# Column units among row units: PV with V as weights, row sums of P by adds on Pool and VectorE

## The chip, the core and the metric

The kernel runs on one core of a Trainium2 chip. Its engines work side by side, each with its own queue, in the order in which the instructions were written into it: TensorE (PE in the profile, its weight loads PEld), VectorE (DVE), ScalarE (ACT), GpSimd (Pool) and SyncE (SP), which here issues most of the DMA transfers. The metric is the device time of one execution in microseconds. Three runs of the kernel before took 1303.82, 1303.84 and 1304.23 us; the median is 1303.84.

## What is computed

Two parts follow each other on x, of 2048 rows by 512 columns: attention with a cached K and V, and a gated MLP that mixes rows. Both are framed by a LayerNorm and a modulation that comes from a small vector c. Cut to what matters here:

```python
h = layernorm(x) * (1 + ca) + sa
q = h @ wq                                  # 32 heads of 128, 2048 rows
scores = q @ k^T * Dh ** (-0.5)             # 4 heads of q share one of 8 K/V groups, 2048 keys
p = softmax(scores, axis=-1)
x = x + ga * ((p @ v) as [2048, 4096] @ wo)
# then: x = x + gb * mixer(layernorm(x) * (1 + cb) + sb)
```

In the kernel the softmax takes no maximum off; it takes exp of the scaled scores, and the sum of each row's exps divides what comes out of PV or of the output projection. A flag at the end guards the sums: if one is out of bounds, the whole is computed again by a general path, which does not run on these inputs.

## The kernel before, in words

Attention is cut into 128 units: 8 K/V groups times 16 tiles of 128 query rows. One unit is 4 heads by 128 queries against 2048 keys, which are 16 key tiles. The loop over `it` has one iteration for each unit's scores, and each iteration has 8 slots. In a slot TensorE does a pair of score matmuls of 512 columns into a PSUM tile of two banks (`s_ps`, two of them), and ScalarE takes the exp of that pair. Into the same slots the loop interleaves PV of an earlier unit (`pv_part`), one matmul of the q projection for a later block (`fill`, slots 0 to 3 of nearly every iteration), and one matmul of the output projection of a still earlier unit (`wo_proj`, slots 4 to 7). The order on each engine's queue is written out by hand: what is emitted first stands first, and `at(it, slot, fn)` puts a function at the head of a later slot. The tile library adds the waits on semaphores and hands out buffers.

There are two kinds of units.

- A row unit keeps q as the weights, so P comes out with queries on partitions (`qk`, line 1021). The exp (line 1028) delivers the sums of its rows by the way, and `turn_rows` adds two halves of them on VectorE (`tot`, line 1082) and takes the reciprocal (line 1085). P has to be turned by a DMA transpose on SP's queue. PV then has V as weights and streams P: 16 matmuls of 512 columns (`pv_rows`, line 1093), which give the output already transposed; VectorE copies it out of PSUM into `oT` (line 1102). As the sums are not yet divided out, each head's output projection goes to a PSUM bank of its own, and VectorE scales and adds it into `xacc` (line 1164).
- A column unit keeps K as the weights, so P comes out with keys on partitions (line 1058, exp at line 1065) and need not be turned. PV takes P as weights, tile by tile, and streams V with a column of ones behind it: 64 matmuls of 129 columns (`pv`, line 1114). The 129th column is the sum. VectorE takes the reciprocals (line 1125) and normalises (line 1126), a DMA transpose turns the result into `oT`, and the four heads of the output projection add up in one PSUM bank, which VectorE adds to `xacc` (line 1158).

Units 5 to 121 repeat row, row, column. A row unit's PV comes 2 or 3 iterations after its scores and a column unit's 1 after, so each iteration holds one PV; the output projection follows 3 iterations behind PV. The iteration after a column unit's therefore has scores of a row unit, PV of the column unit, and the output projection of the column unit before it.

PSUM has eight banks: four for the two `s_ps`, two named `o_ps` for PV, and two named `misc`, which the q projection and the output projection share. The q projection's bank is emptied by VectorE's cast into `qT` (line 970). Pool has next to nothing to do until the last group, when it multiplies and adds the finished rows (lines 1187 and 1188).

Of the kernel before, what the change touches and what calls it, by code (L numbers as in the profile page):

```python
# [10 lines left out]
BF16 = mybir.dt.bfloat16  # L11
FP32 = mybir.dt.float32
ACT = mybir.ActivationFunctionType
ALU = mybir.AluOpType
AX = mybir.AxisListType
P = 128
# [559 lines left out]
def kernel(  # L576
# [19 lines left out]
    nc = tc.nc  # L596
    _, S, D = A_x.shape
    _, HKV, SK, DH = A_k_cache.shape
    HQ = A_wq.shape[1] // DH
    REP = HQ // HKV  # L600
# [4 lines left out]
    NT = S // P  # L605
    NDT = D // P
    NKT = SK // P
# [5 lines left out]
    NSLOT = NKT // 2  # L613
# [26 lines left out]
    res = fast.enter_context(tc.tile_pool(name="res", bufs=1))  # L640
# [4 lines left out]
    late = free_b.enter_context(tc.tile_pool(name="late", bufs=2, side="right"))  # L645
# [24 lines left out]
    def bank(name):  # L670
        return psum.tile([P, 512], FP32, name=name)

    def bank2():
        return psum.tile([P, 1024], FP32, name="s_ps")
# [11 lines left out]
    def normalise(dst, src, mv, rstd):  # L686
        nc.vector.tensor_scalar(
            out=dst,
            in0=src,
            scalar1=mv,  # L690
            scalar2=rstd,
            op0=ALU.subtract,
            op1=ALU.mult,
        )
# [215 lines left out]
    for dt in range(NDT):  # L910
        dst, src = hTs[0][:, dt, 0:P], xT0[:, dt * P : (dt + 1) * P]
        if dt == 1:
            nc.scalar.activation(
                out=dst,
# [67 lines left out]
    def by_rows(u):  # L982
        return TURN_A <= u < TURN_B and (u - TURN_A) % len(LAGS) < len(LAGS) - 1

    row_units = [u for u in range(NU) if by_rows(u)]

    def pv_at(u):
# [15 lines left out]
    def at(it, slot, fn):  # L1003
        later.setdefault((it, slot), []).append(fn)

    def qk(u, i):
        g, j = divmod(u, NT)
        b, jj = g * NCH + j // CT, j % CT
        if i == 0:
            if homes[u] == "wsp":  # L1010
                pTs[u] = wspp.tile([P, NT, 512], BF16, name="wsp")
            else:
                pTs[u] = late.tile([P, NKT, 512], BF16, name=homes[u], bufs=1)
            if by_rows(u):
                rsums[u] = stat.tile([P, NSLOT], FP32, name="rs")
        s_ps = bank2()
        if by_rows(u):
            hh, half = divmod(i, 2)
            for c in range(2):
                k0 = (2 * half + c) * 512  # L1020
                nc.tensor.matmul(  # L1021
                    s_ps[:, c * 512 : (c + 1) * 512],
                    lhsT=qTs[b][:, hh, jj * P : (jj + 1) * P],
                    rhs=groups[g]["kT"][:, k0 : k0 + 512],
                    start=True,
                    stop=True,
                )
            nc.scalar.activation(  # L1028
                out=rows_of(u, hh)[:, half * HK : (half + 1) * HK],
                in_=s_ps[:],  # L1030
                func=ACT.Exp,
                scale=inv_sqrt_dh,
                accum_out=rsums[u][:, i : i + 1],
            )
            if half == 1:
                at(*divmod(u * NSLOT + i + 1, NSLOT), lambda: turn_rows(u, hh))
            return
        if u < 2:
            pair, k0 = i // 4, i % 4 * 4
            qs = slice(pair * 256, (pair + 1) * 256)  # L1040
            for kt in range(4):
                nc.tensor.matmul(  # L1042
                    s_ps[:, kt * 256 : (kt + 1) * 256].rearrange("p (r q) -> p r q", r=2),
                    lhsT=groups[g]["kT"][:, (k0 + kt) * P : (k0 + kt + 1) * P],
                    rhs=qTs[b][:, 2 * pair : 2 * pair + 2, jj * P : (jj + 1) * P],
                    start=(kt % 2 == 0),
                    stop=(kt % 2 == 1),
                )
            nc.scalar.activation(
                out=pTs[u][:, k0 : k0 + 4, qs],  # L1050
                in_=s_ps[:].rearrange("p (k q) -> p k q", k=4),
                func=ACT.Exp,
                scale=inv_sqrt_dh,
            )
            return
        for h in range(2):
            kt = 2 * i + h
            nc.tensor.matmul(  # L1058
                s_ps[:, h * 512 : (h + 1) * 512].rearrange("p (r q) -> p r q", r=REP),
                lhsT=groups[g]["kT"][:, kt * P : (kt + 1) * P],  # L1060
                rhs=qTs[b][:, :, jj * P : (jj + 1) * P],
                start=True,
                stop=True,
            )
        nc.scalar.activation(  # L1065
            out=pTs[u][:, 2 * i : 2 * i + 2, :],
            in_=s_ps[:].rearrange("p (k q) -> p k q", k=2),
            func=ACT.Exp,
            scale=inv_sqrt_dh,
        )  # L1070

    def rows_of(u, hh):
        return pn[(row_units.index(u) * REP + hh) % len(pn)][:, 0:SK]
# [71 lines left out]

    def wo_proj(u):
        g, j = divmod(u, NT)
        each = by_rows(u)
        ps = {}

        def into(first, X_ps, scale):
            if first:
                xaccs[j] = late.tile([P, D], FP32, name=f"xacc{j}", bufs=1)
            xa = xaccs[j]
            if scale is None and first:
                nc.vector.tensor_copy(out=xa[:], in_=X_ps[:])
            elif scale is None:
                nc.vector.tensor_tensor(out=xa[:], in0=X_ps[:], in1=xa[:], op=ALU.add)
            elif first:
                nc.vector.tensor_scalar(  # L1160
                    out=xa[:], in0=X_ps[:], scalar1=scale, scalar2=None, op0=ALU.mult
                )
            else:
                nc.vector.scalar_tensor_tensor(  # L1164
                    out=xa[:], in0=X_ps[:], scalar=scale, in1=xa[:], op0=ALU.mult, op1=ALU.add
                )

        def mm(hh):
            if hh == 0 or each:
                ps[0] = bank("misc")  # L1170
            nc.tensor.matmul(  # L1171
                ps[0][:],
                lhsT=oTs[u][:, hh, :],
                rhs=groups[g]["wo"][:, hh, :],
                start=(hh == 0 or each),
                stop=(hh == REP - 1 or each),
            )
            if each:
                c0 = u * REP + hh
                into(g == 0 and hh == 0, ps[0], rall[:, c0 : c0 + 1])  # L1180
            elif hh == REP - 1:
                into(g == 0, ps[0], None)
            if hh < REP - 1 or g < HKV - 1:
                return
            xa = xaccs[j]
            engine = nc.gpsimd if j < NT - CT else nc.vector
            engine.tensor_tensor(out=xa[:], in0=xa[:], in1=ga_rows[:], op=ALU.mult)
            engine.tensor_tensor(
                out=x_sb[:, j, :], in0=xa[:], in1=x_sb[:, j, :], op=ALU.add
            )  # L1190
            if j >= NT - CT:
                ln_stats(mv2, j, x_sb[:, j, :])

        return [lambda hh=hh: mm(hh) for hh in range(REP)]

    def ln2(it, j):

        st = {}

        def first():  # L1200
            if j < NT - CT:
                ln_stats(mv2, j, x_sb[:, j, :])
            st["rstd"] = rstd_of(mv2[:, j : j + 1, :], 1, "ln2")

        def second():
            xn = res.tile([P, D], BF16, name="xn2", bufs=2)
            normalise(xn[:], x_sb[:, j, :], mv2[:, j, 0:1], st["rstd"][:, 0:1])
            st["xnT"] = res.tile([P, NDT, P], BF16, name="xnT2", bufs=2)
            nc.sync.dma_start_transpose(out=st["xnT"][:], in_=xn[:])

        def third():
            ch, c0 = j // CT, (j % CT) * P
            if ch not in h2Ts:
                h2Ts[ch] = res.tile([P, NDT, 512], BF16, name="hT", bufs=NCH)
            for dt in range(NDT):
                nc.vector.tensor_scalar(
                    out=h2Ts[ch][:, dt, c0 : c0 + P],
                    in0=st["xnT"][:, dt, :],
                    scalar1=modc[:, 4 * NDT + dt : 4 * NDT + dt + 1],
                    scalar2=modc[:, 3 * NDT + dt : 3 * NDT + dt + 1],  # L1220
                    op0=ALU.mult,
                    op1=ALU.add,
                )

        at(it + 1, 0 if j >= NT - CT else 2, first)
        at(it + 1, 4, second)
        at(it + 2, 3, third)
# [44 lines left out]
        first[j] = ln1_stats(j, 1)  # L1272

    def tile_norm(j):
        xn = res.tile([P, D], BF16, name="xn2", bufs=2)
        normalise(xn[:], x_sb[:, j, :], mv1[:, j, 0:1], first[j][:, 0:1])
        first[j] = xn

# [193 lines left out]
        at(NU + 5, 5 + ch, lambda ch=ch: z2_norm(ch))  # L1472

    def pv_part(u, i, n):
        if by_rows(u):
            return pv_rows(u, i, n)
        for k in range(NSLOT // n):
            pv(u, i * (NSLOT // n) + k)
# [250 lines left out]
```

## Time and profile before

| | |
|---|---|
| median of three runs | 1303.84 us |
| profiled execution | 1303.83 us |
| its span, first to last instruction | 1302.0 us |
| TensorE busy | 1287.0 us, 99% |
| ScalarE busy | 1112.8 us, 85% |
| VectorE busy | 685.7 us, 53% |
| Pool busy | 59.0 us, 5% |
| main DMA queue, share of 16 engines | 87.5% |

The page of a profile gives busy times of each engine, the chain of work that ended last, and the costliest groups of instructions. A timeline row gives the start in microseconds from the span's start, the duration, engine, line, operation, what is written and read with the shape, and how many instructions were merged; in brackets stands the idle time of that engine before it and what ended it. A row of groups gives the count, the busy time, the mean duration of one in nanoseconds, and after the last bar the idle time ahead of them. A matmul's duration reaches to the modelled end of its way through the array; the next starts earlier than that, so time on TensorE is best read from one start to another.

### The profile page before, as it was taken

The numbers are of one execution on the slowest core, as the hardware profiler recorded it, in microseconds if no ns is written. First come the engines' busy times: TensorE is split into PE (matmuls) and PEld (weight loads), VectorE is DVE, ScalarE is ACT, GpSimd is POOL, SyncE is SP. The second block draws the span as 40 slices with busy tenths as digits, with TensorE's granted clock in tenths as the row PEclk, the third lists the DMA queues.
The fourth block names the chain that finished last, engine by engine and source line by source line (L and its number), as shares of the span: only waits on it lengthen the run. The fifth ranks groups of instructions, "written<-read, shape, count | busy, mean of one in ns | idle before, by whom it ended". The sixth has DMA issues, their size and how long they took to land.

```text
span 1302.0 us, 22572 instructions
## 1 busy us (share of the span) xinstructions
PE 1287.0 (99%) x8512; PEld 700.2 (54%) x8665; DVE 685.7 (53%) x1777; ACT 1112.8 (85%) x1683; POOL 59.0 (5%) x99
## 2 busy tenths in 40 slices
PE   9999999999999999999999999999999999999998
PEld 7655555555555555555555555555555556644445
DVE  7545455545554555455545554555455566784444
ACT  7999999999999999999999999999999998650000
POOL 2000000000000000000000000000000133410000
PEclk9999999999999999999999999999999999999999
DMA  7999999999999999999999999999999973254300
GB/s 207 183 188 181 168 184 191 190 166 188 189 181 177 186 174 189 183 171 188 190 175 181 187 192 181 169 195 173 176 193 165 172 146 91 49 138 98 81 21 32
DMA packets 774997, 211.18 MB, mean 162 GB/s; under 512 B 759264, under 2 KB 773216, under 8 KB 774880
## 3 DMA queue, kind: packets, MB, share of 16 engines
q1 hardware_dynamic: 772864, 207.94, 87.5%
q10 hardware_dynamic: 2016, 1.71, 0.4%
q8 instruction: 70, 1.15, 0.4%
q14 instruction: 47, 0.39, 0.1%
HBM read 21.37 MB, written 2.10 MB: 18 GB/s over the span
## 4 chain that ended last, share of the span: by engine, by line
PE 98%; issue 1%; ACT 1%; DMA 0%; SPq 0%; DVE 0%; ACTq 0%
PE s_ps L1021 21%; PE o_ps L1093 20%; PE o_ps L1114 14%; PE s_ps L1058 13%; PE misc L1171 8%; PE misc L959 8%; PE misc L1573 7%; PE s_ps L1397 2%; PE s_ps L1436 2%; PE o_ps L1606 1%; PE s_ps L1042 0%; PE s_ps L1606 0%; DMA kT<-in_A_k_cache_dram 0%; ACT pn L1028 0%; ACT win_sb L1028 0%
## 5 line engine op out<-in xcount | busy, mean ns | idle before, releaser
L1021 PE MATMUL s_ps<-kT,qT 128*128 128x512 bf16 x1219 | 365.0, 379 | 2.3
L1028 ACT ACTIVATE win_sb<-s_ps 128x1024 bf16<-128x1024 f32 x312 | 319.0, 1023 | 3.4 <-PE s_ps L1021 0.7
L1093 PE MATMUL o_ps<-pT,v 128*128 128x512 bf16 x909 | 272.6, 379 | 1.5
L1164 DVE SCALAR_TENSOR_TENSOR xacc<-misc,rall,xacc 128x512 f32<-128x512 f32 x304 | 227.5, 748 | 69.2 <-PE misc L1171 61.7
L1058 PE MATMUL s_ps<-qT,kT 128*128 128x512 bf16 x768 | 228.4, 379 | 0.8
L1065 ACT ACTIVATE pT<-s_ps 128x1024 bf16<-128x1024 f32 x208 | 209.8, 1024 | 11.8 <-PE s_ps L1058 3.6
L1028 ACT ACTIVATE pn<-s_ps 128x1024 bf16<-128x1024 f32 x208 | 212.7, 1023 | 2.3 <-PE s_ps L1021 0.7
L1093 PEld LDWEIGHTS <-v 128*128 128x128 bf16 x1248 | 121.9, 98 | 147.9 <-issue 1.1
L1065 ACT ACTIVATE wsp<-s_ps 128x1024 bf16<-128x1024 f32 x176 | 179.8, 1023 | 12.4 <-PE s_ps L1058 4.6
L1171 PE MATMUL misc<-wo_g,oT 128*128 128x512 bf16 x479 | 181.6, 379 | 1.0
L1021 PEld LDWEIGHTS <-qT 128*128 128x128 bf16 x1248 | 121.4, 98 | 109.4 <-issue 0.4
L959 PE MATMUL misc<-hT,wq_g 128*128 128x512 bf16 (+1 forms) x499 | 178.3, 369 | 0.5
L970 DVE CAST qT<-misc 128x512 bf16<-128x512 f32 x126 | 86.5, 687 | 153.5 <-PE misc L959 153.5
L1114 PEld LDWEIGHTS <-pT 128*128 128x128 bf16 x1792 | 119.6, 98 | 48.8
L1082 DVE TENSOR_TENSOR tot<-rs 128x1 f32<-128x1 f32 x312 | 48.4, 155 | 171.3 <-ACT win_sb L1028 114.9
L1114 PE MATMUL o_ps<-v,pT 128*128 128x129 bf16 x1792 | 137.5, 220 | 0.6
L1058 PEld LDWEIGHTS <-kT 128*128 128x128 bf16 x768 | 74.1, 98 | 81.1 <-issue 1.1
L1114 PEld LDWEIGHTS <-wsp 128*128 128x128 bf16 x1408 | 94.3, 98 | 41.5
L1114 PE MATMUL o_ps<-v,wsp 128*128 128x129 bf16 x1408 | 108.5, 220 | 0.5
L1028 ACT ACTIVATE wmod_a<-s_ps 128x1024 bf16<-128x1024 f32 x104 | 106.3, 1023 | 0.6 <-PE s_ps L1021 0.4
L1573 PE MATMUL misc<-wsp,z 128*128 128x512 bf16 (+2 forms) x554 | 100.1, 336 | 0.3
L1093 PE MATMUL o_ps<-wsp,v 128*128 128x512 bf16 x292 | 87.8, 379 | 0.4
(118 smaller groups left out, 894.6 us busy)
## 6 DMA issues: line engine op xcount, KB each, us to landing
wo_g<-in_A_wo_dram SPq DMA_DIRECT2D x8, 512.0 KB, 4.5
wq_g<-in_A_wq_dram SPq DMA_DIRECT2D x7, 512.0 KB, 4.1
v<-in_A_v_cache_dram SPq DMA_DIRECT2D x7, 512.0 KB, 4.7
wsp<-in_w_mod_dram SPq DMA_DIRECT2D x1, 2048.0 KB, 9.1
pT<-win_sb SPq DMA_TRANSPOSE x117, 5.0
win_sb<-in_B_w_in_dram SPq DMA_DIRECT2D x1, 1792.0 KB, 7.3
x_sb<-in_A_x_dram SPq DMA_DIRECT2D x3, 512.0 KB, 7.0
out_dram<-yout ACTq DMA_DIRECT2D x12, 128.0 KB, 1.7
```

The source lines that it names most:

```text
L959: nc.tensor.matmul(ps[0][:, o0 : o0 + n], lhsT=wqs[g][:, dt, hh * DH : (hh + 1) * DH], rhs=hTs[ch][:, dt, c0 : c0 + n], start=(dt == 0), s ...
L970: nc.vector.tensor_copy(out=dst, in_=src)
L1021: nc.tensor.matmul(s_ps[:, c * 512 : (c + 1) * 512], lhsT=qTs[b][:, hh, jj * P : (jj + 1) * P], rhs=groups[g]["kT"][:, k0 : k0 + 512], sta ...
L1028: nc.scalar.activation(out=rows_of(u, hh)[:, half * HK : (half + 1) * HK], in_=s_ps[:], func=ACT.Exp, scale=inv_sqrt_dh, accum_out=rsums[u ...
L1058: nc.tensor.matmul(s_ps[:, h * 512 : (h + 1) * 512].rearrange("p (r q) -> p r q", r=REP), lhsT=groups[g]["kT"][:, kt * P : (kt + 1) * P], ...
L1065: nc.scalar.activation(out=pTs[u][:, 2 * i : 2 * i + 2, :], in_=s_ps[:].rearrange("p (k q) -> p k q", k=2), func=ACT.Exp, scale=inv_sqrt_dh,)
L1082: nc.vector.tensor_tensor(out=tot[:], in0=rs[:, 2 * hh : 2 * hh + 1], in1=rs[:, 2 * hh + 1 : 2 * hh + 2], op=ALU.add)
L1093: nc.tensor.matmul(o_pss[u][:], lhsT=groups[g]["v1"][:, kt, 0:DH], rhs=pTs[u][:, kt, :], start=(kt == 0), stop=(kt == NKT - 1),)
L1114: nc.tensor.matmul(o_ps[:, hh % 2, 0 : DH + 1], lhsT=pTs[u][:, kt, hh * P : (hh + 1) * P], rhs=groups[g]["v1"][:, kt, 0 : DH + 1], start=( ...
L1164: nc.vector.scalar_tensor_tensor(out=xa[:], in0=X_ps[:], scalar=scale, in1=xa[:], op0=ALU.mult, op1=ALU.add)
L1171: nc.tensor.matmul(ps[0][:], lhsT=oTs[u][:, hh, :], rhs=groups[g]["wo"][:, hh, :], start=(hh == 0 or each), stop=(hh == REP - 1 or each),)
L1573: nc.tensor.matmul(g_pss[f][:, :n], lhsT=z2[:, st, f * P : (f + 1) * P], rhs=wsp[t][:, st, c0 : c0 + n], start=(st == 0), stop=(st == NT - ...
```

## The change

For the 35 column units u = 7, 10, ... 109 (`by_sums`), PV is done as for row units: V as weights, P streamed in 16 matmuls of 512 columns, the result copied straight into `oT`. The normalising operations on VectorE, the DMA transpose of `onorm` and the column of ones go out of use for them, and their output projection becomes one PSUM bank and one scaled add on VectorE per head.

The sums of P are made by adds. Pool adds key tiles 0 to 11 into one float tile of 128 x 512 (11 operations, emitted in slots 1 to 6 of the unit's own iteration), VectorE adds tiles 12 to 15 into another (3 operations, at the head of slots 0, 1 and 2 of the next iteration). Pool joins the two into a bf16 tile (`join`), and in slot 2 of the iteration after that four matmuls of one column, with this tile as weights and ones streamed, add it over the partitions (`close`); VectorE takes the reciprocals. The two float tiles (`acc`) take the place of the second LayerNorm's buffers, which now live in tiles of the same name.

In the excerpts of the change, lines of `add`'s and `close`'s arguments are shortened to one line.

```diff
+    def by_sums(u):
+        return TURN_A <= u < (HKV - 1) * NT and not by_rows(u)
...
+            if by_sums(u):
+                key_sums(u)
...
+    N_POOL = 12
+
+    def key_sums(u):
+        acc = [res.tile([P, D], FP32, name="acc", bufs=2) for _ in range(2)]
+        pT = pTs[u]
+
+        def add(engine, a, kt, first):
+            engine.tensor_tensor(out=a[:],
+                in0=pT[:, first, :] if kt == first + 1 else a[:], in1=pT[:, kt, :], op=ALU.add)
+
+        for kt in range(1, N_POOL):
+            at(*divmod(u * NSLOT + kt // 2 + 1, NSLOT), lambda kt=kt: add(nc.gpsimd, acc[0], kt, 0))
+        for kt, (unit, slot) in zip(range(N_POOL + 1, NKT), ((1, 0), (1, 1), (1, 2))):
+            at(u + unit, slot, lambda kt=kt: add(nc.vector, acc[1], kt, N_POOL))
+
+        def join():
+            onorms[u] = late.tile([P, REP, P], BF16, name="onorm", bufs=3)
+            nc.gpsimd.tensor_tensor(out=onorms[u][:], in0=acc[0][:]..., in1=acc[1][:]..., op=ALU.add)
+
+        def close():
+            t_ps = bank("o_ps")
+            for hh in range(REP):
+                nc.tensor.matmul(t_ps[:, hh : hh + 1], lhsT=onorms[u][:, hh, :],
+                    rhs=ones_bf[:, 0:1], start=True, stop=True)
+            nc.vector.reciprocal(out=rall[:, u * REP : (u + 1) * REP], in_=t_ps[:, 0:REP])
+
+        at(u + 1, 4, join)
+        at(u + 2, 2, close)
...
     def wo_proj(u):
         g, j = divmod(u, NT)
-        each = by_rows(u)
+        each = by_rows(u) or by_sums(u)
...
     def pv_part(u, i, n):
-        if by_rows(u):
+        if by_rows(u) or by_sums(u):
             return pv_rows(u, i, n)
```

More of the change, by code (lines that the diff above doesn't have):

```diff
@@ L1070, in qk @@
         )
+    N_POOL = 12
[3 more added lines that the diff above has]
+        def add(engine, a, kt, first):
+            engine.tensor_tensor(
+                out=a[:],
+                in0=pT[:, first, :] if kt == first + 1 else a[:],
+                in1=pT[:, kt, :],
+                op=ALU.add,
+            )
+        for kt in range(1, N_POOL):
[4 more added lines that the diff above has]
+            onorms[u] = late.tile([P, REP, P], BF16, name="onorm", bufs=3)
+            nc.gpsimd.tensor_tensor(
+                out=onorms[u][:],
+                in0=acc[0][:].rearrange("p (r q) -> p r q", r=REP),
+                in1=acc[1][:].rearrange("p (r q) -> p r q", r=REP),
+                op=ALU.add,
+            )
+        def close():
+            t_ps = bank("o_ps")
+            for hh in range(REP):
+                nc.tensor.matmul(
+                    t_ps[:, hh : hh + 1],
+                    lhsT=onorms[u][:, hh, :],
+                    rhs=ones_bf[:, 0:1],
+                    start=True,
+                    stop=True,
+                )
+            nc.vector.reciprocal(out=rall[:, u * REP : (u + 1) * REP], in_=t_ps[:, 0:REP])
+        at(u + 1, 4, join)
+        at(u + 2, 2, close)
     def rows_of(u, hh):
@@ L1205, in second @@
         def second():
[L1206 to L1209, printed above, removed]
+            both = res.tile([P, D], FP32, name="acc", bufs=2)[:].bitcast(BF16)
+            xn = both[:, 0:D]
+            normalise(xn, x_sb[:, j, :], mv2[:, j, 0:1], st["rstd"][:, 0:1])
+            st["xnT"] = both[:, D : 2 * D].rearrange("p (d q) -> p d q", d=NDT)
+            nc.sync.dma_start_transpose(out=st["xnT"], in_=xn)
         def third():
@@ L1274, in tile_norm @@
     def tile_norm(j):
-        xn = res.tile([P, D], BF16, name="xn2", bufs=2)
+        xn = res.tile([P, D], FP32, name="acc", bufs=2)[:].bitcast(BF16)[:, 0:D]
         normalise(xn[:], x_sb[:, j, :], mv1[:, j, 0:1], first[j][:, 0:1])
```

## The prediction

> **What bounds the kernel now.** I read the page's busy times and its chain first, then the engines' timelines through one period of the attention stage, then the groups by shape. The profiled execution took 1303.83 us, of which 1302.0 are the span; it agrees with the median of the runs, 1303.84, so sums against it stand as they are. About 0.2% (2.6 us) is what a measurement of this kernel can tell from no change.
>
> ```profile
> span 1302.0 us, 22572 instructions
> PE 1287.0 (99%) x8512; PEld 700.2 (54%) x8665; DVE 685.7 (53%) x1777; ACT 1112.8 (85%) x1683; POOL 59.0 (5%) x99
> PE 98%; issue 1%; ACT 1%; DMA 0%; SPq 0%; DVE 0%; ACTq 0%
> ```
>
> TensorE is the bound, without gaps. Whatever takes a microsecond out of its stream saves one, and whatever makes it wait costs one. VectorE is half idle and Pool almost wholly: the work that the change gives them is free on average, and costs only where TensorE waits for it. So the question is which of their instructions TensorE waits for, and when.
>
> The order repeats every three units: two row units, one column unit. One unit's scores take 8 slots. Call the iteration of a column unit's own scores C, and the next two R1 and R2. R1 holds the column unit's PV. From TensorE's timeline (start us, duration, what, count):
>
> ```profile
> 605.22 0.59 PE L1021 MATMUL s_ps<-kT,qT 128*128 128x512 bf16 x2
> 613.85 0.59 PE L1058 MATMUL s_ps<-qT,kT 128*128 128x512 bf16 x2
> 620.11 0.38 PE L1171 MATMUL misc<-wo_g,oT 128*128 128x512 bf16 x1
> 622.49 0.59 PE L1021 MATMUL s_ps<-kT,qT 128*128 128x512 bf16 x2
> 622.92 0.62 PE L1114 MATMUL o_ps<-v,pT 128*128 128x129 bf16 x8
> 631.29 0.59 PE L1021 MATMUL s_ps<-kT,qT 128*128 128x512 bf16 x2
> ```
>
> C starts at 613.85, R1 at 622.49 and the next R2 at 631.29. With a row unit's PV inside, an iteration lasts 622.49 - 613.85 = 8.64 us (605.22 to 613.85: 8.63); R1, with the 64 narrow PV matmuls, 8.80. In a row-PV iteration the second output matmul (slot 5) stands at 620.11, 6.26 us after the start. I need this below.
>
> **The change, part by part.**
>
> *PV of 35 column units* (u = 7, 10, ... 109): 64 matmuls of 129 columns become 16 of 512, so R1 should shrink to the others' length: 8.80 - 8.64 = 0.16 us, 35 times, -5.6 us.
>
> *Four one-column matmuls per unit* come in on TensorE. The nearest row is the modulation's, 16 of the same form:
>
> ```profile
> 59.02 0.54 PE L839 MATMUL o_ps<-sc_bf,wsp 128*128 128x1 bf16 x16
> 59.42 0.59 PE L1021 MATMUL s_ps<-kT,qT 128*128 128x512 bf16 x2
> ```
>
> 16 take 59.42 - 59.02 = 0.40 us, 25 ns each, so four take 0.10 us; 35 times +3.5 us. TensorE's own gain is therefore only 0.06 us a unit, 2.1 in all. They use an o_ps bank, and the built program gives them the one that the column unit's PV left a slot or two earlier, and the PV two iterations later takes that one again: no bank is asked for while its copy is running, so I take nothing for it (had it been the other bank, the 0.69 us oT copy would stick out by some 0.3 us, 10 us in all).
>
> *Moved off:* 35 transposes of onorm leave SP's queue and 35 x (2 reciprocals, 2 normalising operations) leave VectorE. The chain has DMA at 0% and SP's queue at 0%, so this gains nothing; nothing else is moved past a queue. The exps and the row units' transposes stay. LayerNorm's buffers at the end merely change their name and share a tile, at the same depth: nothing.
>
> *Output projection of these units:* each head now has its own PSUM bank and its own VectorE operation (748 ns) in place of one sum (681). It falls into R1, slots 4 to 7, as the row units' does elsewhere at one slot each without holding TensorE up. But two misc banks now alternate in R1 between the q projection (slots 0 to 3) and the four heads. The second head's matmul takes the bank that the q cast (L970) has to empty, the third the bank of the first head's L1164. Before, one bank served all four heads. So in R1 TensorE newly waits for VectorE's queue at slot 5, 6.26 us in.
>
> *What now stands in that queue before the q cast:* three adds of P (L1084 in the changed kernel) and the row sum "tot". And Pool does 11 adds and a join. The prices, from the groups by shape (busy us, mean ns of one):
>
> ```profile
> L1164 DVE SCALAR_TENSOR_TENSOR xacc<-misc,rall,xacc 128x512 f32<-128x512 f32 x304 | 227.5, 748 | 69.2 <-PE misc L1171 61.7 <-PE s_ps L1058 0.9
> L970 DVE CAST qT<-misc 128x512 bf16<-128x512 f32 x126 | 86.5, 687 | 153.5 <-PE misc L959 153.5
> L1102 DVE CAST oT<-o_ps 128x512 bf16<-128x512 f32 x78 | 53.9, 691 | 11.9 <-PE o_ps L1093 3.6
> L1085 DVE RECIPROCAL rall<-tot 128x1 f32<-128x1 f32 x312 | 51.1, 164 | 10.8
> L1082 DVE TENSOR_TENSOR tot<-rs 128x1 f32<-128x1 f32 x312 | 48.4, 155 | 171.3 <-ACT win_sb L1028 114.9 <-ACT pn L1028 55.4
> L1158 DVE TENSOR_TENSOR xacc<-misc,xacc 128x512 f32<-128x512 f32 x42 | 28.6, 681 | 3.6 <-PE misc L1171 2.4 <-PE s_ps L1058 1.2
> L1065 ACT ACTIVATE pT<-s_ps 128x1024 bf16<-128x1024 f32 x208 | 209.8, 1024 | 11.8 <-PE s_ps L1058 3.6
> L1187 POOL TENSOR_TENSOR xacc<-xacc,ga_rows 128x512 f32<-128x512 f32 x12 | 15.3, 1276 | 215.6 <-DVE xacc L1158 180.4 <-DVE xacc L1164 35.2
> L1188 POOL TENSOR_TENSOR x_sb<-xacc,x_sb 128x512 bf16<-128x512 f32 x12 | 13.8, 1154 | 0.9
> L1187 DVE TENSOR_TENSOR xacc<-xacc,ga_rows 128x512 f32<-128x512 f32 x4 | 2.8, 692 | 0.1
> ```
>
> A VectorE add is 0.69 us (its L1187). A Pool add lies between 1.15 and 1.28 us (float and bf16 inputs, with a bf16 or a float output); I take 1.22. Added up without interference, R1's queue is fine: 3 x 0.69 = 2.1 us of adds start about 1.3 us in and end by 3.4, before the q cast is even due (4.5 us in: 618.37 - 613.85, below).
>
> Interference is what decides, and the trace shows it where Pool's L1187/L1188 run beside VectorE:
>
> ```profile
> 1022.84 1.27 POOL L1187 TENSOR_TENSOR xacc<-xacc,ga_rows 128x512 f32<-128x512 f32 x1 [165.43 <-DVE xacc L1158]
> 1024.18 1.15 POOL L1188 TENSOR_TENSOR x_sb<-xacc,x_sb 128x512 bf16<-128x512 f32 x1
> 1048.96 1.27 POOL L1187 TENSOR_TENSOR xacc<-xacc,ga_rows 128x512 f32<-128x512 f32 x1 [4.30 <-DVE xacc L1158]
> 1057.68 1.27 POOL L1187 TENSOR_TENSOR xacc<-xacc,ga_rows 128x512 f32<-128x512 f32 x1 [4.31 <-DVE xacc L1164]
> ```
>
> ```profile
> 1021.72 0.16 DVE L1082 TENSOR_TENSOR tot<-rs 128x1 f32<-128x1 f32 x1 [1.46 <-ACT pn L1028]
> 1023.73 0.39 DVE L1082 TENSOR_TENSOR tot<-rs 128x1 f32<-128x1 f32 x1
> 1024.25 0.75 DVE L1164 SCALAR_TENSOR_TENSOR xacc<-misc,rall,xacc 128x512 f32<-128x512 f32 x1
> 1049.85 0.40 DVE L1082 TENSOR_TENSOR tot<-rs 128x1 f32<-128x1 f32 x1
> 1058.55 0.41 DVE L1082 TENSOR_TENSOR tot<-rs 128x1 f32<-128x1 f32 x1
> ```
>
> The one-element "tot", both of whose inputs are in SBUF, takes 0.16 us alone, but 0.39, 0.40 and 0.41 where it falls into a Pool operation, and ends each time with it: 1024.12 against Pool's 1024.11, 1050.25 against 1050.23, 1058.96 against 1058.95. L1164, with one input in PSUM, runs its usual 0.75 beside Pool's L1188. So a VectorE operation with two SBUF inputs waits out Pool's running operation, and goes through in the 0.07 us gap behind it (1024.11 to 1024.18). The Trainium skill says this too ("SBUF — State Buffer", section "Who interferes with whom"): a VectorE instruction with two SBUF inputs contends with a Pool instruction that reads SBUF, and whoever is first holds the shared pair for the whole instruction. The three rows agree with it for VectorE waiting; that Pool waits in its turn no row here shows. By that page's rule the sum is the one taken below; without such blocking it would be the second rival's.
>
> The new adds are just of this kind, and Pool is busy right there. When Pool starts, and when VectorE comes to the adds:
>
> ```profile
> 614.48 8.58 ACT L1065 ACTIVATE pT<-s_ps 128x1024 bf16<-128x1024 f32 x8
> ```
>
> ```profile
> 618.37 0.69 DVE L970 CAST qT<-misc 128x512 bf16<-128x512 f32 x1 [2.92 <-PE misc L959]
> 622.47 0.69 DVE L1102 CAST oT<-o_ps 128x512 bf16<-128x512 f32 x1
> 623.08 0.74 DVE L1164 SCALAR_TENSOR_TENSOR xacc<-misc,rall,xacc 128x512 f32<-128x512 f32 x1
> ```
>
> The eight exps of C start 0.63 us in; the first ends 1.02 us later (L1065 above), 1.65 us in, and the others follow at about 1.08. Pool's adds then follow each other at 1.22 + 0.07 = 1.29 us, slower than the exps feed them (one exp for two adds): the n-th starts 1.75 + 1.29(n - 1) us after C's start, the 11th ends near 16 us, which is 7.2 us into R1 even undisturbed. VectorE comes free for the first P add when L1164 ends, 623.82, or 1.3 us into R1 = 9.95 after C's start. Pool's 7th add runs from 9.5 to 10.7. Hence, in us after R1's start: add 1 waits until 2.07 and ends 2.76; it must finish before the dependent add 2 goes out, and Pool, which has been held for this time, takes its 8th add: 3.98; add 2 ends 4.67; Pool's 9th 5.89; add 3 6.58; Pool's 10th 7.80; tot and reciprocal 8.15; q cast 8.84, with handovers 8.9. TensorE wanted that bank at 6.26: it stands 2.65 us. Behind it, the next tot waits out Pool's 11th add (to 9.2), then reciprocal and the first head's L1164 until about 10.3, where TensorE, 8.9 + 5 matmuls of 0.216 (8.64 us over 40), arrives at 10.0: another 0.3 us. Pool's join then ends near 10.5 us into R1, 3 us before the four small matmuls, so they wait for nothing. The next unit that writes this P tile does so in R2's slot 2, later still.
>
> TensorE cannot catch up, so a period costs 2.65 + 0.3 - 0.06 = 2.9 us. The first of the 35 has no such neighbour for its banks (unit 4, in the output stage of that iteration, keeps its one bank); 34 x 2.9 = 98 us. Sum: 1303.8 + 98 = 1402.
>
> Both ends of the blocking: with Pool at 1.15 us and VectorE arriving as an add ends, the cast ends at 1.3 + 2.07 + 3.45 + 0.35 + 0.69 + 0.1 = 7.96, a stall of 1.7 + 0.3 - 0.06 = 1.95 us, 66 in all: 1370. With 1.28 and a full add to wait first: 1.3 + 1.28 + 2.07 + 3.84 + 0.35 + 0.69 + 0.1 = 9.6, 3.35 + 0.3 - 0.06 = 3.6, 122 in all: 1426.
>
> **The rivals.**
>
> *VectorE's three adds go in one turn.* If VectorE keeps the way open and Pool gets in only after add 3, the cast ends at 2.07 + 2.07 + 1.22 (one Pool add before tot) + 0.35 + 0.69 = 6.4, a stall of 0.15, and the first head's operation 0.3 late: 0.45 - 0.06 = 0.4 us, 34 times 13: 1317. For it: VectorE's next instruction is ready in its queue. Against: each add reads what the last wrote, and the rows show VectorE itself slipping into a 0.07 us gap of Pool, so a waiting engine is quick.
>
> *No blocking that matters; ends on the other side.* The blocked tots lost only 0.25 us each, and all three met L1187, which reads two float inputs; if a long add shares with Pool, the cast ends by 5.2 us (618.37 + 0.69 - 613.85), a microsecond before TensorE asks. It decides as soon as VectorE is done with adds and tot by 5.5 us. Then only TensorE's own 0.06 x 35 remain: 1303.8 - 2.1 = 1301.7, not slower, and too little to be told from no change; were the four small matmuls hidden altogether, 1298.
>
> *Pool itself becomes late.* Eleven adds, held three times by 0.69, leave it some 3 us before the small matmuls. If contention stretches its adds to 1.6 us, these 12 operations take 4.6 us more, TensorE's stall at slot 5 grows by three of them, 1.1 us, and the small matmuls may wait as well: about 4.3 us a period, 34 times 146: 1450.
>
> **How the numbers follow.** Blocking in turns 0.68; three adds in one turn 0.15; no blocking 0.10; Pool late 0.07. The likeliest gives 1402, by itself 1370 to 1426. Its band holds most of its 0.68, and with the one-turn case 8 in 10 need 1314 to 1428. Only the third case is not slower; of its 0.10, 0.06 fall within 0.2% and 0.04 below. So faster 0.04, same 0.06, slower 0.90.
>
> **What would show it.** Right: in R1, TensorE idle some 2.5 us ahead of a misc matmul of the output projection, released by VectorE's L970; the VectorE adds in L1084 recorded at well over 0.69 us (1.5 to 2), Pool's near 1.9 where they meet; iterations C and R2 still 8.6. The four small matmuls 0.1 us and unwaited; no wait of TensorE for an o_ps copy. TensorE's busy time nearly unchanged, the span longer. Wrong: VectorE's adds at 0.69 beside Pool's at 1.2, or all three within one Pool add; a TensorE wait on Pool's join, or on L1150; or a misc bank free at slot 5 in spite of late adds.

## The result, and the profile after

The changed kernel takes 1344.99 us (1344.92 to 1345.09), against 1303.83 for the kernel before in the same comparison: a ratio of 1.0314, 95% interval 1.0300 to 1.0327. It is slower, as forecast, and at the place forecast, but by 41 us and not by 98.

The page of the changed kernel, its busy times:

```profile
span 1343.1 us, 20375 instructions
PE 1296.8 (97%) x6998; PEld 631.3 (47%) x7125; DVE 926.6 (69%) x1917; ACT 1112.8 (83%) x1683; POOL 582.1 (43%) x519
```

TensorE's busy time went up by 10 us only (a matmul's modelled end also covers the first 0.16 us of a wait: 0.90 us idle below where the wait is 1.06); the span grew by 41.1. TensorE now has gaps. The list of waits (who waited for whom: us in total, times, the longest) has one new row of weight on TensorE:

```profile
PE misc L1219 <- DVE qT L970: 31.2, 34, 1.2
```

34 times the output projection waits for VectorE's q cast, which is the place and the count that the prediction had. One period on TensorE's timeline; 629.09 is the start of an R2, 637.82 of a C, 646.46 of an R1:

```profile
626.51 0.38 PE L1219 MATMUL misc<-wo_g,oT 128*128 128x512 bf16 x1 [0.90 <-DVE qT L970]
629.09 0.59 PE L1026 MATMUL s_ps<-kT,qT 128*128 128x512 bf16 x2
631.25 0.24 PE L1108 MATMUL o_ps<-ones_bf,onorm 128*128 128x1 bf16 x4
631.35 0.59 PE L1026 MATMUL s_ps<-kT,qT 128*128 128x512 bf16 x2
637.82 0.59 PE L1063 MATMUL s_ps<-qT,kT 128*128 128x512 bf16 x2
646.46 0.59 PE L1026 MATMUL s_ps<-kT,qT 128*128 128x512 bf16 x2
653.78 0.38 PE L1219 MATMUL misc<-wo_g,oT 128*128 128x512 bf16 x1 [0.90 <-DVE qT L970]
655.07 0.38 PE L1219 MATMUL misc<-wo_g,oT 128*128 128x512 bf16 x1
```

From one waiting matmul to the next is 653.78 - 626.51 = 27.27 us; before, a period was 631.29 - 605.22 = 26.07. C still takes 646.46 - 637.82 = 8.64, and R2 637.82 - 629.09 = 8.73, which is 8.63 and the 0.10 us of the four small matmuls (631.25 to 631.35). So R1 takes 27.27 - 8.64 - 8.73 = 9.90 us. It should have been 8.64. The matmul at 653.78 was due at 646.46 + 6.26 = 652.72: it is 1.06 us late; the next head's, at 655.07, is due 5 x 0.216 after it, 654.86: another 0.21. That is 1.27 us where the prediction had 2.95.

VectorE and Pool in that R1:

```profile
647.05 0.74 DVE L1212 SCALAR_TENSOR_TENSOR xacc<-misc,rall,xacc 128x512 f32<-128x512 f32 x1
647.71 1.08 DVE L1084 TENSOR_TENSOR acc<-pT 128x512 f32<-128x512 bf16 x1
648.89 1.46 DVE L1084 TENSOR_TENSOR acc<-acc,pT 128x512 f32<-128x512 f32 x1
650.38 1.53 DVE L1084 TENSOR_TENSOR acc<-acc,pT 128x512 f32<-128x512 f32 x1
651.83 1.11 DVE L1130 TENSOR_TENSOR tot<-rs 128x1 f32<-128x1 f32 x1
653.06 0.67 DVE L970 CAST qT<-misc 128x512 bf16<-128x512 f32 x1
```

```profile
647.08 2.72 POOL L1084 TENSOR_TENSOR acc<-acc,pT 128x512 f32<-128x512 f32 x2
648.32 3.05 POOL L1084 TENSOR_TENSOR acc<-acc,pT 128x512 f32<-128x512 f32 x2
649.88 3.04 POOL L1084 TENSOR_TENSOR acc<-acc,pT 128x512 f32<-128x512 f32 x2
651.44 1.48 POOL L1084 TENSOR_TENSOR acc<-acc,pT 128x512 f32<-128x512 f32 x1
653.00 1.15 POOL L1084 TENSOR_TENSOR acc<-acc,pT 128x512 f32<-128x512 f32 x1
```

(A Pool row marked x2 holds two adds, of which the second is also the first of the next row; so the starts of the five adds are those of the five rows, and the end of such a row is the end of its second add.) The turns are there: add, Pool add, add, Pool add, add, Pool add, tot. Each of VectorE's operations ends shortly after one of Pool's: Pool's add of 648.32 ended at 649.80 (647.08 + 2.72), and VectorE's second add at 650.35, 0.55 later; the tot ends at 652.94, 0.02 after Pool's add of 651.44 (652.92). And Pool waits in its turn, which the trace of before could not show: its adds start 1.56 us apart here (648.32, 649.88, 651.44, 653.00) against 1.24 before the adds meet (647.08 to 648.32), and one takes 1.48 in place of 1.15. But a turn of both engines costs 1.56 us: from the end of Pool's add at 649.80 to the end of VectorE's at 650.35 is 0.55, and from there to the end of Pool's next, at 651.37 (648.32 + 3.05), 1.02. The prediction counted 0.69 + 1.22 = 1.91.

### The profile page after: what moved, and what is told of

Same layout as the page of the kernel before. It is cut to its first block, busy times and chain, and to the rows that moved or that the text cites. A ratio compares the mean times of both kernels' runs of the same rounds, so it can differ in the third digit from the quotient of the medians.

```text
span 1343.1 us, 20375 instructions
## 1 busy us (share of the span) xinstructions
PE 1296.8 (97%) x6998; PEld 631.3 (47%) x7125; DVE 926.6 (69%) x1917; ACT 1112.8 (83%) x1683; POOL 582.1 (43%) x519
## 5 line engine op out<-in xcount | busy, mean ns | idle before, releaser
L1212 DVE SCALAR_TENSOR_TENSOR xacc<-misc,rall,xacc 128x512 f32<-128x512 f32 x441 | 328.9, 746 | 72.7 <-PE misc L1219 61.6
L1141 PE MATMUL o_ps<-pT,v 128*128 128x512 bf16 x1174 | 352.1, 379 | 1.7
L1141 PEld LDWEIGHTS <-v 128*128 128x128 bf16 x1808 | 176.6, 98 | 213.6
L1084 POOL TENSOR_TENSOR acc<-acc,wsp 128x512 f32<-128x512 f32 x180 | 225.6, 1254 | 14.1
L1219 PE MATMUL misc<-wo_g,oT 128*128 128x512 bf16 x501 | 189.7, 379 | 33.7 <-DVE qT L970 31.2
L1084 POOL TENSOR_TENSOR acc<-acc,pT 128x512 f32<-128x512 f32 x170 | 213.1, 1254 | 13.3
L1141 PE MATMUL o_ps<-wsp,v 128*128 128x512 bf16 x575 | 172.4, 379 | 0.7
L1084 POOL TENSOR_TENSOR acc<-wsp 128x512 f32<-128x512 bf16 x18 | 20.7, 1152 | 218.2 <-ACT wsp L1070 218.2
L1130 DVE TENSOR_TENSOR tot<-rs 128x1 f32<-128x1 f32 x312 | 95.8, 307 | 24.0 <-ACT win_sb L1033 16.6
L1084 POOL TENSOR_TENSOR acc<-pT 128x512 f32<-128x512 bf16 x17 | 19.6, 1152 | 193.0 <-ACT pT L1070 193.0
```

The costliest lines, as they stand in the source:

```text
L1084: engine.tensor_tensor(out=a[:], in0=pT[:, first, :] if kt == first + 1 else a[:], in1=pT[:, kt, :], op=ALU.add,)
L1130: nc.vector.tensor_tensor(out=tot[:], in0=rs[:, 2 * hh : 2 * hh + 1], in1=rs[:, 2 * hh + 1 : 2 * hh + 2], op=ALU.add)
L1141: nc.tensor.matmul(o_pss[u][:], lhsT=groups[g]["v1"][:, kt, 0:DH], rhs=pTs[u][:, kt, :], start=(kt == 0), stop=(kt == NKT - 1),)
L1212: nc.vector.scalar_tensor_tensor(out=xa[:], in0=X_ps[:], scalar=scale, in1=xa[:], op0=ALU.mult, op1=ALU.add)
L1219: nc.tensor.matmul(ps[0][:], lhsT=oTs[u][:, hh, :], rhs=groups[g]["wo"][:, hh, :], start=(hh == 0 or each), stop=(hh == REP - 1 or each),)
```

## The experiments

Two theories had to be told apart. By turns: VectorE's adds are slow, and the q cast with them, because each waits out a Pool add. By load: Pool does not matter; three adds and four scaled adds are too much in front of TensorE in one iteration. The first three runs take parts away, the fourth moves one add to Pool; all four are compared with the kernel before on the same chip (1304.0 us there). The last four ran on another chip, where the kernel before took 1303.77 us.

**VectorE's adds without Pool's.**

```diff
-        for kt in range(1, N_POOL):
-            at(..., lambda kt=kt: add(nc.gpsimd, acc[0], kt, 0))
...
-                in0=acc[0]...
+                in0=acc[1]...
```

> Leaves out Pool's 11 adds (the sums then cover key tiles 12 to 15 only); VectorE's three adds, the join, the four small matmuls, the new PV and the output projection per head stay. By turns (VectorE's adds are slow because each waits out a Pool add): the adds take 0.69 us, end some 3.4 us into the iteration, the q cast is in time, TensorE has no wait on it, 1302 us. By load (three adds and four scaled adds are simply too much for VectorE's queue in that iteration): the same wait as in the changed kernel, about 1345.

Measured 1301.38 us, ratio 0.9979 (0.9969 to 0.9989). VectorE's adds by groups (mean ns after the bar's busy us), in the changed kernel and then in this run:

```profile
L1084 DVE TENSOR_TENSOR acc<-acc,wsp 128x512 f32<-128x512 f32 x36 | 53.8, 1493 | 2.5
```

```profile
L1084 DVE TENSOR_TENSOR acc<-acc,wsp 128x512 f32<-128x512 f32 x36 | 24.9, 692 | 2.5
```

These 36 of the 70 adds into acc (the group of 34 shows the same) take 692 ns in the same queue and not 1493, and TensorE's wait on the q cast is gone. The load theory falls.

**Pool's adds without VectorE's.**

```diff
-        for kt, (unit, slot) in zip(range(N_POOL + 1, NKT), ((1, 0), (1, 1), (1, 2))):
-            at(u + unit, slot, lambda kt=kt: add(nc.vector, acc[1], kt, N_POOL))
...
-                in1=acc[1]...
+                in1=acc[0]...
```

> Leaves out VectorE's three adds (key tiles 12 to 15 are missing from the sums; the join adds Pool's tile to itself); all else as in the changed kernel. By turns: only the row sums tot still wait out Pool's adds, up to 1.2 us each; the q cast still ends before TensorE asks for its bank (6.26 us in), 1302 us. If Pool's running alone slows other engines, or its blocking of the tots is enough, the wait at the second head's matmul stays in part: 1310 or more.

Measured 1301.32 us, ratio 0.9979 (0.9969 to 0.9989). Pool's adds alone cost nothing either, though they still hold up the row sums. Pool's adds and "tot" in this run, and the same Pool group in the changed kernel:

```profile
L1084 POOL TENSOR_TENSOR acc<-acc,wsp 128x512 f32<-128x512 f32 x180 | 207.8, 1155 | 14.1
L1128 DVE TENSOR_TENSOR tot<-rs 128x1 f32<-128x1 f32 x312 | 64.7, 207 | 78.8 <-ACT win_sb L1033 51.7 <-ACT pn L1033 26.4 <-ACT wmod_a L1033 0.2
```

```profile
L1084 POOL TENSOR_TENSOR acc<-acc,wsp 128x512 f32<-128x512 f32 x180 | 225.6, 1254 | 14.1
```

Either half of the adds is free; only the two together cost some 44 us (1344.99 - 1301.4 = 43.6; the kernel before agrees within 0.2 us between the two comparisons).

**No sums at all, only the new PV.**

```diff
-            if by_sums(u):
-                key_sums(u)
...
+    nc.vector.memset(rall[:], 1.0)
```

> Leaves out all of the sums of P (no adds, no join, no small matmuls; their reciprocals are set to 1), keeps the new PV and the output projection per head. Both theories: TensorE saves 0.16 us in each of 35 iterations and waits for nothing, 1303.8 - 5.6 = 1298.2. If the scaled adds per head were what fills VectorE's queue, a wait at the second or third head's matmul would be left: over 1304.

Measured 1298.05 us, ratio 0.9952 (0.9935 to 0.9969). TensorE's saving is what was predicted: 1304.0 - 1298.05 = 5.95 us against 5.6. And from here to the two runs above, which have the four small matmuls, is 3.3 us (1301.35 - 1298.05) against 3.5.

**One turn less.**

```diff
-    N_POOL = 12
+    N_POOL = 13
```

> One key tile more to Pool: 12 adds there, two on VectorE; nothing left out. In the changed kernel's trace each VectorE add in turn with Pool costs 1.56 us of time. By turns: with one turn less the q cast ends 1.56 us earlier, 5.7 us into the iteration, before it is asked for at 6.26: no wait, about 1302. By load: one add of 0.69 us less, the wait shrinks from 1.05 to 0.4 us: about 1318.

Measured 1302.53 us, ratio 0.9988 (0.9978 to 0.9998). No wait of TensorE on the q cast is left in its list. One add moved from VectorE to Pool takes 42 us off the changed kernel. VectorE in an R1 of this run, whose first score matmul stands at 621.49:

```profile
621.47 0.69 DVE L1150 CAST oT<-o_ps 128x512 bf16<-128x512 f32 x1
622.74 1.08 DVE L1084 TENSOR_TENSOR acc<-pT 128x512 f32<-128x512 bf16 x1
623.85 1.53 DVE L1084 TENSOR_TENSOR acc<-acc,pT 128x512 f32<-128x512 f32 x1
625.30 1.11 DVE L1130 TENSOR_TENSOR tot<-rs 128x1 f32<-128x1 f32 x1
626.53 0.67 DVE L970 CAST qT<-misc 128x512 bf16<-128x512 f32 x1
```

The cast ends at 627.20, 5.71 us in; in the changed kernel it ended at 653.73 - 646.46 = 7.27. One turn is 1.56 us, and 5.71 lies before the 6.26 at which TensorE asks. This run stands 1.2 us above the two runs with one half of the adds. From the start of one column unit's scores to the next it takes 26.02 us where those two take 26.00, which makes about half of that over 35 units; what holds it up there stays open.

**Six half adds.** Is the price of a turn paid per operation or by the amount of data?

```diff
+        def half(kt, hf):
+            cols = slice(hf * D // 2, (hf + 1) * D // 2)
+            nc.vector.tensor_tensor(out=acc[1][:, cols], in0=..., in1=pT[:, kt, cols], op=ALU.add)
...
-            at(u + unit, slot, lambda kt=kt: add(nc.vector, acc[1], kt, N_POOL))
+            for hf in range(2):
+                at(u + unit, slot, lambda kt=kt, hf=hf: half(kt, hf))
```

> VectorE's three adds are cut into six of 256 columns each; the same sums, the same data. By turns, where each add costs a whole Pool add however short it is: Pool's 7th to 11th add each let one half in, the q cast ends some 9.0 us into the iteration in place of 7.3, TensorE waits 1.8 us longer in 34 iterations: 1345 + 63 = 1408 (more, if the join gets in front of the row sum). If the two engines share the port in proportion to data: six halves cost what three wholes do, with some 0.1 us for each instruction more, 1345 to 1356.

Measured 1422.94 us, ratio 1.0914 (1.0892 to 1.0936). The same data in twice as many operations costs 78 us more. VectorE's six halves in one R1 (x2 and x4), and Pool's adds beside them (rows marked x2 overlap as above):

```profile
694.90 2.11 DVE L1095 TENSOR_TENSOR acc<-pT 128x256 f32<-128x256 bf16 x2
696.93 4.29 DVE L1095 TENSOR_TENSOR acc<-acc,pT 128x256 f32<-128x256 f32 x4
```

```profile
694.27 2.45 POOL L1084 TENSOR_TENSOR acc<-acc,pT 128x512 f32<-128x512 f32 x2
695.51 2.51 POOL L1084 TENSOR_TENSOR acc<-acc,pT 128x512 f32<-128x512 f32 x2
696.80 2.51 POOL L1084 TENSOR_TENSOR acc<-acc,pT 128x512 f32<-128x512 f32 x2
698.09 2.51 POOL L1084 TENSOR_TENSOR acc<-acc,pT 128x512 f32<-128x512 f32 x2
699.39 1.22 POOL L1084 TENSOR_TENSOR acc<-acc,pT 128x512 f32<-128x512 f32 x1
```

The six halves take 694.90 to 701.22, 6.3 us; the three wholes took 647.71 to 651.91, 4.2. Sharing by data is out. The first five halves wait out a Pool add each; at the sixth Pool's adds are done (700.61). A turn with a half add is 1.29 us (Pool's starts: 695.51, 696.80, 698.09, 699.39), with a whole one 1.56, without one 1.24. From end to end, a half adds 0.29 us to Pool's end (694.27 + 2.45 = 696.72 to 694.90 + 2.11 = 697.01) where a whole added 0.55, and Pool's next add ends 1.01 us after it (695.51 + 2.51 = 698.02), as it did after a whole one. So in a turn VectorE's part goes by its columns, and Pool's stays. Both parts, 0.55 and 1.01, are some 0.14 us shorter than the durations that the two have alone, 0.69 and 1.15; that much of each seems to run while the other still holds it up. Their sum is the 1.56; the 1.91 had the whole 0.69, and 1.22 for a Pool add.

The expectation of 1408 for this run missed 15 us, and that it came so near is partly luck. It took the wait to grow by 1.8 us. In the 11 units in which TensorE keeps its full clock, it is 28.58 us from one column unit's scores to the next, against 27.27 in the changed kernel: 1.3 us more, which in 34 units would give about 1390 by estimate. The rest of the time is a lower clock of TensorE in the other 23, which is told below.

**VectorE's adds after Pool's.**

```diff
-        for kt, (unit, slot) in zip(range(N_POOL + 1, NKT), ((1, 0), (1, 1), (1, 2))):
-            at(u + unit, slot, lambda kt=kt: add(nc.vector, acc[1], kt, N_POOL))
+        for kt in range(N_POOL + 1, NKT):
+            at(u + 2, 0, lambda kt=kt: add(nc.vector, acc[1], kt, N_POOL))
...
-        at(u + 1, 4, join)
-        at(u + 2, 2, close)
+        at(u + 2, 4, join)
+        at(u + 3, 2, close)
```

> VectorE's three adds stand at the head of the iteration after, when Pool's 11 are done; the join and the four small matmuls follow correspondingly later; nothing left out. By turns: the adds meet no Pool operation, take 0.69 us each, no wait of TensorE: as without them, 1301.3. By load: the same work in front of the same kind of queue (q cast, four scaled adds), the wait merely moves to that iteration: 1330 to 1345.

Measured 1301.43 us, ratio 0.9982 (0.9972 to 0.9991). All of the work of the changed kernel is done; only the two engines' adds no longer meet. This gives back all of the 44 us, and VectorE's adds are at 692 ns again. So it is the meeting of the two, and not the amount of work, that cost the time.

**Sums over partitions without TensorE.** What is left is the 3.3 us of the small matmuls.

```diff
-    N_POOL = 12
+    N_POOL = 13
...
+        def turn_sums():
+            tT = late.tile([P, REP, P], BF16, name="onorm", bufs=3)
+            nc.sync.dma_start_transpose(out=tT[:], in_=onorms[u][:].rearrange("p r q -> p (r q)"))
+            onorms[u] = tT
+
         def close():
-            t_ps = bank("o_ps")
-            for hh in range(REP): nc.tensor.matmul(t_ps[:, hh : hh + 1], lhsT=onorms[u][:, hh, :], ...)
-            nc.vector.reciprocal(out=rall[:, u * REP : (u + 1) * REP], in_=t_ps[:, 0:REP])
+            tots = stat.tile([P, REP], FP32, name="tots")
+            nc.vector.tensor_reduce(out=tots[:], in_=onorms[u][:], axis=AX.X, op=ALU.add)
+            nc.vector.reciprocal(out=rall[:, u * REP : (u + 1) * REP], in_=tots[:])
...
-        at(u + 2, 2, close)
+        at(u + 2, 3, turn_sums)
+        at(u + 3, 3, close)
```

> 12 adds on Pool and 2 on VectorE, and in place of the four small matmuls a DMA transpose of the joined sums and a VectorE sum along the free axis; nothing left out. If the small matmuls cost 0.10 us a unit and nothing else is left on TensorE: 1302.5 - 3.5 = 1299. If the transpose on SP's queue holds the row units' transposes up, or VectorE's sum is in front of something TensorE waits for: 1302 or more.

Measured 1298.68 us (1298.61 to 1298.79), ratio 0.9961 (0.9947 to 0.9975). It beats both kernels: 5.1 us below the kernel before, 0.6 above the run without any sums. Against the run with one turn less, from which it differs in the sum over partitions alone, it is 3.9 us shorter (3.5 expected), and from one column unit's scores to the next it takes 25.92 us and not 26.02.

**Both together.**

> VectorE's three adds after Pool's, and the sum over partitions by DMA transpose and VectorE; nothing left out. By turns, no contention and no small matmuls: what the run without any sums took, 1298.1; otherwise between that and 1302.

The edit is that of the last two runs together, but with Pool's 11 adds and VectorE's three of the changed kernel, and with the transpose in slot 7 of the iteration after next and the sum in slot 5 of the one behind it. Measured 1302.08 us, ratio 0.9988 (0.9978 to 0.9997): a miss. VectorE's sum now often stands waiting for its transpose, with the heads' scaled adds behind it. Its waits, here and then in the faster run:

```profile
DVE tots L1114 <- DMA onorm<-onorm: 10.9, 15, 2.3
PE misc L1220 <- DVE xacc L1213: 2.6, 2, 1.7
```

```profile
DVE tots L1114 <- DMA onorm<-onorm: 4.4, 8, 1.5
```

Here most units take 25.90 us from one column unit's scores to the next, as in the run without any sums. In seven of the 35, one matmul of the output projection, the last head's beside a column unit's scores, is late by 0.14 to 1.86 us, 4.0 us in all, and that is about the whole difference from the run without any sums (1302.08 - 1298.05). Each of the seven stands behind a sum that waited for its transpose. (The list holds the two longest alone, and without the part that a matmul's modelled end covers.) That is a wait at the head of VectorE's queue once more, this time for a DMA.

## Why the prediction was wrong

- *TensorE's gain*, 0.16 us a unit for PV and 0.10 for the small matmuls: right (5.95 us against 5.6, 3.3 against 3.5).
- *No gain from SP's queue, nothing lost at the o_ps banks, no wait on Pool's join*: right. There is no such wait in the list, and R2 grew by the 0.10 us alone.
- *Where it would hurt*: right. R1, the second head's matmul, held by the q cast behind the blocked adds, 34 times; a smaller wait at the third head (0.21 us, 0.3 predicted). That VectorE and Pool take turns, and that Pool waits too, is what the runs with one half of the adds, and with the two apart in time, show.
- *The term that was mis-sized* is "add 1 waits until 2.07 and ends 2.76; ... takes its 8th add: 3.98; add 2 ends 4.67; ..." It adds full recorded durations of two engines that alternate, 0.69 + 1.22 = 1.91 a turn. A turn measured 1.56. Three of them make 1.05 us, and Pool's adds at 1.15 (1.24 apart) and not at 1.22 (1.29) bring the first turn forward by some 0.3. Another 0.3 lies behind the turns: from the end of Pool's 10th add to the end of the cast it took 0.81 us (652.92 to 653.73) and not 1.10, as the tot ended with that add. So the cast ended at 7.27 and not at 8.9. The wait is only what sticks out beyond 6.26, so 1.6 us less of queue is 60% less of wait: 1.06 and not 2.65. The sum with the measured terms: 1.06 + 0.21 - 0.06 = 1.21, 34 times, 41 us.
- The rows shown in the prediction held the correction. The blocked tots ended 0.01 to 0.02 us after Pool's operation although one takes 0.15 by itself: nearly all of a tot's own time had already passed when Pool's operation ended. The same 0.14 us or so is what a whole add saves, 0.55 in place of 0.69. I used these rows for whether there is blocking, and not for what a turn costs. So the lower end, 1370, was too high as well: it varied Pool's duration and the phase, but kept the 0.69. The 1345 lies between 1314 and 1428 only because that range was drawn down to the one-turn rival, whose mechanism did not come; that is luck.
- *Rivals*: three adds in one turn, and no blocking, are both refuted by the rows of VectorE and Pool above. Pool's adds did come 1.56 us apart where they meet VectorE's, close to the third rival's 1.6, but only in three turns of a unit: the small matmuls did not wait for the join. Of the signs, Pool's adds were expected near 1.9 us where they meet VectorE's and were recorded at 1.48; TensorE's gap was expected at some 2.5 and was 0.9. (A slip in the working, 9.95 us after C's start for what its rows give as 9.97, changes nothing.)

## What to carry to other kernels

An idle engine is not a free one if its operations take turns with another's: put VectorE's operations with two SBUF inputs where Pool is quiet, and count them as operations, since a short one waits out a Pool operation as a long one does (the row sum above took 1.11 us and not 0.15). When two engines take turns, price the turn from one start to the next, not from the sum of the durations that each has alone. And where a wait is the part of a queue that sticks out beyond a due time, give the due time and the queue separate bounds: here a single operation less in the queue was worth 42 us.

## What was not expected of the hardware

In the run with half adds TensorE's wait was 2.1 to 2.4 us in the records, and behind 23 of its 34 waits the clock fell to half for about 3.4 us. TensorE's timeline at the first of them, and two stretches of 3.5 us there with busy times by engine, the granted clock ahead of the last two columns:

```profile
109.46 0.38 PE L1229 MATMUL misc<-wo_g,oT 128*128 128x512 bf16 x1 [2.21 <-DVE qT L970]
110.10 1.06 PE L1151 MATMUL o_ps<-pT,v 128*128 128x512 bf16 x2
113.95 0.59 PE L1151 MATMUL o_ps<-wsp,v 128*128 128x512 bf16 x2
```

```profile
106.50:110.00 3.50, 1.29 (x7) 0.52 (x6) 3.43 (x8) 1.53 (x4) 2.61 (x3) 1.00 1.10 197
110.00:113.50 3.50, 3.50 (x10) 1.21 (x8) 2.60 (x7) 2.08 (x4) 0.00 (x0) 0.51 0.84 157
```

Two matmuls take 1.06 us in place of 0.59 while the clock is low. Over the stage from 75 to 985 us the clock of that run is 0.96, and 4% of 910 us is some 36 us, by estimate about half of the 78 us that this run has over the changed kernel. In the changed kernel, with a wait of 0.9 us in the records, it stays at 1.00. The Trainium skill ("TensorE: Matmul & The Clock Gate", section "HAM oscillation — how this bites in real kernels") gives as the rule that idle gaps of more than about 3.4 us are to be avoided; here gaps of 2.1 to 2.4 us were enough in 23 cases, and in 11 others, of 2.1 us as well, the clock stayed; what decides between them no run here shows. So the wait of 2.65 us that was predicted would probably have cost more than its own length in many of the units.

The Trainium skill ("SBUF — State Buffer", section "Who interferes with whom") says that the engine that comes second is blocked for the whole instruction of the first. The order of the turns agrees with it in every row above; the price does not follow from the recorded durations, since a turn takes 1.56 us and not 0.69 + 1.15 = 1.84.
